# Residual and stores of the first half beside its inverse, a second store queue and a third PSUM pair at the end of an S4 and MLP mixer

## The chip, the cores and the metric

The kernel runs on one core of a Trainium2 chip. Its engines are TensorE (PE), VectorE (DVE), ScalarE (ACT), GpSimd (POOL) and SyncE (SP), each with an instruction stream of its own; they meet through semaphores. SP only issues DMAs here. PE writes PSUM (eight banks of 128 partitions x 2 KB), the other work happens in SBUF, and inputs, output and scratch are in HBM. The metric is the device time of one execution in microseconds, as a median of several.

## What is computed: the reference, cut short

```python
def reference(A_u, ...):
    x = A_u                                   # (1, 2048, 512) f32
    xn = _layernorm(x)
    s = _A_ref(xn, ...)      # S4: K[d, l] = Re sum_n C exp(dt A l) dt B
                             # s = irfft(rfft(xn) * rfft(K)) + xn * Dskip
    g = _silu(_B_ref(xn, B_w1, B_w2, B_w3, B_w4))
    return x + s * g

def _B_ref(x, w1, w2, w3, w4):
    h = _gelu(_layernorm(x) @ w1)             # 512 -> 512
    x1 = x + shift(h) @ w2                    # four channel groups moved by +1, -1, +2, -2 rows
    return x1 + _gelu(_layernorm(x1) @ w3) @ w4   # 512 -> 1376 -> 512
```

The convolution along the 2048 positions, its kernel K, the MLP, the gate and the residual are all within the time.

## The kernel before

**Layout.** X is one SBUF tile of [128, 16, 512] f32: position index (t r s) has s (16 values) in the middle dimension and (r t) on the 128 partitions; the channels are split into two halves of DH = 256 (hf = 0 and 1). X holds the normalized input first, then x1, then the MLP's result, then its Silu, then the product with the convolution, and at last the sum that is stored.

**Stages, as the program lists them.** (1) `loads`, `params`, `token_mixing`: the inputs come in, the first MLP (w1, w2) runs, the input of the convolution goes to DRAM as scr_Ud, and w3, w4 are cut into f16 parts. (2) `tables(hf)`: 16 blocks of 32 channels make the convolution's kernel. ACT computes exponentials (mag) and sines, DVE forms the tables pt and kt (128x2080), PE sums them in pc, and the result goes to scr_Kd. (3) `kstage1(hf)` loads ksl from scr_Kd, transforms it (`pd<-ksl,ks`), copies it to k1e and stores scr_Kf. (4) `products(hf)`: loads kin, uin and cst; PE transforms, DVE multiplies the spectra (pr), PE goes half way back (`pd<-pr,cst`), copies z1e are stored to scr_Zda or scr_Zdb. (5) `mlp(g)`, g = 0 to 7, each for two values of s (1024 columns of X): `pb<-x1T,w3h` matmuls in f16, Gelu to g, g rounded into f16 ghl and its remainder, `pa<-w4h,ghl` matmuls, and `X<-pa,wsc,X` adds them to X. (6) `gate(g)`: Silu on ACT, 128x1024. (7) `inverse(hf, g)`, 16 units: one DMA loads zin, 16 matmuls `p?<-zin,is` fill a pair of PSUM banks, and two DVE products of 128x256 multiply X by them. Such a unit of 16 matmuls with its pair of products is what the text calls a unit. The pair of banks comes from `pp_pair`, which alternates between banks 2 and 3, named pc and pd (pc0, pc1 are the two tiles of one pair). (8) `finish(g)`: every second g loads x again into xr ([128, 4, 512], four DMAs by `by_r`, one per group of 32 partitions), DVE adds 128x1024 of it to X, and four DMAs store the result to out_dram, all on SP's queue Q.

**What sets the order.** None of this is issued as written. `Plan` records every instruction with its reads and writes, and `Plan.order` is a list scheduler: it simulates the engines with planned costs (`pe_cost`, `act_cost`, `dve_cost`, 0.45 us for a DMA issue on SP, LAND for a transfer's landing), and of the instructions that are ready gives each engine the one with the lowest due time. A due time is the base of a stage (T0 + TC * cc for a table block, M0 + MC * g for an MLP group, KA, KB, PA, PB, FA, FB for the others) plus an entry of SHIFT, which has one number for each call of `due`. Copies and some roundings (`E.copy`, `E.affine`) may go to ACT or DVE; PREFER and AVOID say which. So an instruction's place comes from numbers, and each engine then runs its stream in that order. In the profile every instruction carries the line of the helper that issues it, L310 before and L314 after; instructions are told apart by their tiles.

**Places that the text speaks of.** `pp_pair` (line 559), `due` (571), `by_r` (577), `inverse` (893), `finish` (910), the rings of buffers zinr and the places xrs (543, 544). zinr[0] has five buffers of 4 KB per partition for the zin of the first half, zinr[1] eight for the second.

Of the kernel before, what the change touches and what calls it, by code (L numbers as in the profile page):

```python
# [10 lines left out]
F32 = mybir.dt.float32  # L11
# [8 lines left out]
P = 128  # L20
L = 2048
D = 512
# [61 lines left out]
class Op:  # L84
# [10 lines left out]
SAME = {"PE": 0.0, "ACT": 0.13, "DVE": 0.1, "SP": 0.0}  # L95
TABLE_LOAD = 1.41
DMA_RATE = 300e3
LAND, PAD = 2.45, 0.16
BASE, FINE, END = 16512, 19840, 229368

KGC, QUAD = 3.25, 0.95
WARM = 40

SHIFT = (
# [21 lines left out]
)  # L126
Q0, QC = -778.0, 0.05
SWITCH = 2279.26
PREFERP, AVOIDP = 2674.41, 272.51
PREFER, AVOID = 3332.92, 790.65  # L130
PV, T0, TC = 257.0, 396.7, 309.52
LX, LC, LP, LW, LV = -4000.0, 0.11, -3964.6, -2693.7, -3696.7
M0, MC, WC = 807.9, 710.86, 0.25
H0, HC, SC = -3530.1, 638.4, 0.22
KA, PA, PAC, FA = -1045.1, -3015.7, 0.25, 592.1
KB, PB, PBC, FB = -157.1, -136.4, 0.08, 323.0
FC = 0.29


def mlp_due(g, jp):  # L140
# [3 lines left out]
class Plan:  # L144
# [105 lines left out]
    def order(self):  # L250
# [17 lines left out]
        while len(out) < len(ops):  # L268
# [4 lines left out]
            for o in pools[e]:  # L273
                if o.ready <= t + 0.02:
                    v = o.vt
                    if e == "ACT" and o.table and o.table != table:
                        v += SWITCH
                    if len(o.alts) > 1:
# [37 lines left out]
def is_ap(x):  # L316
    return hasattr(x, "tensor") and hasattr(x, "ap")


def columns(ap):  # L320
    n = 1
    for s in ap.shape[1:]:
        n *= s
    return n


def pe_cost(name, args):
    f = 1 if args[2].dtype == F16 else 4
    return 0.11 if name == "transpose" else columns(args[2]) * f / 2400.0 + 0.0025 * (1 + f // 4)


def act_cost(args, kw):
    small = sum(1 for k in ("bias", "scale") if is_ap(kw.get(k)))
    cost = columns(args[0]) * (0.00075 if "PSUM" in str(args[1].space) else 0.00084) + 0.092 + 0.088 * small
    return cost + (0.11 if is_ap(kw.get("accum_out")) else 0.0)
# [19 lines left out]
class Engine:  # L355
# [3 lines left out]
    def __getattr__(self, name):  # L359
        def call(*args, **kw):  # L360
            aps = [a for a in args if is_ap(a)] + [kw[k] for k in ("bias", "scale") if is_ap(kw.get(k))]
            writes, reads = aps[:1], aps[1:]
            if is_ap(kw.get("accum_out")):
                writes = writes + [kw["accum_out"]]
            if name == "matmul" and not kw["start"]:
                reads = reads + writes
            table, nbytes = 0, 0
            if self.eng == "PE":
                cost = pe_cost(name, args)
            elif self.eng == "ACT":  # L370
                cost = act_cost(args, kw)
                if name == "activation":
                    table = TABLES.get(args[2], 0)
            elif self.eng == "DVE":
                cost = dve_cost(name, args)
            else:
                cost = 0.45
                nbytes = 4 * min(columns(a) * a.shape[0] for a in aps)
            self.plan.add({self.eng: (cost, (name, args, kw))}, writes, reads, table, nbytes)

        return call
# [38 lines left out]
def kernel(  # L420
# [9 lines left out]
    V, A, T, Q = [Engine(plan, e) for e in ("DVE", "ACT", "PE", "SP")]  # L430
    E = Either(plan)

    xv = u[0].rearrange("(t r s) d -> r t s d", r=4, s=S)
    ov = out[0].rearrange("(t r s) d -> r t s d", r=4, s=S)
# [5 lines left out]
    DH = D // 2  # L440
# [13 lines left out]
    def at(offset, shape, dt, name):  # L454
        return nc.alloc_sbuf_tensor_at(name, shape, dt, offset=offset)[:]
# [37 lines left out]
    X = at(area(4 * S * D), [P, S, D], F32, "X")  # L493
    K2, K4 = 2048, 4096
# [8 lines left out]
    early = area(11 * K2)  # L503
# [25 lines left out]
    o = late + 8 * K4  # L529
# [10 lines left out]
        ),  # L540
    ]

    zinr = [Ring(early, K4, 5), Ring(o, K4, 8)]
    xrs = [late + 2 * K4 * k for k in range(3)] + [o + 10 * K4]
    assert o + 12 * K4 <= END

# [1 line left out]
    bank = [[ps.tile([P, D], F32, name=f"p{n}{i}") for i in range(2)] for n in "abcd"]  # L548
    turn = {"mm": 0, "kg": 0, "pp": 0, "t": 0}
# [6 lines left out]
        turn["kg"] += 1  # L556
        return bank[2][turn["kg"] % 2]

    def pp_pair():
        turn["pp"] += 1  # L560
        return bank[2 + turn["pp"] % 2]

    def t_bank():
        turn["t"] += 1
# [6 lines left out]
    def due(t=None):  # L571
        plan.stage += 1
        t = plan.base = plan.base if t is None else t
        plan.vt = t + (SHIFT[plan.stage] if plan.stage < len(SHIFT) else 0)


    def by_r(sb, dr, to_dram=False):

        for r in range(4):
            a, d = sb[32 * r : 32 * r + 32], dr[r]  # L580
            Q.dma_start(d, a) if to_dram else Q.dma_start(a, d)

    w1s, w2s = [], []

# [303 lines left out]
    def gate(g):  # L888
        due(FA + FC * g)
        X2 = X[:, 2 * g : 2 * g + 2]  # L890
        A.activation(X2, X2, AF.Silu)

    def inverse(hf, g):
        due((FA, FB)[hf] + FC * g)
        ch = slice(hf * DH, hf * DH + DH)
        zin = zinr[hf]([P, 4, DH], F32, "zin")
        Q.dma_start(zin, Zd[hf][:, 2 * g : 2 * g + 2, :, :, :].rearrange("r s e g d -> (s e g) r d"))
        py = [t[:, :DH] for t in pp_pair()]
        with plan.together(cost=0.55):
            for r in range(4):  # L900
                for a in range(2):
                    h = slice(64 * a, 64 * a + 64)
                    T.matmul(py[a][32 * r : 32 * r + 32], is2[h], zin[h, r], start=True, stop=True)
        for a in range(2):
            Xh = X[:, 2 * g + a, ch]
            V.tensor_mul(Xh, Xh, py[a])

    xr = []

    def finish(g):  # L910
        due(FB + FC * g)
        if g % 2 == 0:
            xr.append(at(xrs.pop(), [P, 4, D], F32, "xr"))
            by_r(xr[-1], xv[:, :, 2 * g : 2 * g + 4])
        X2 = X[:, 2 * g : 2 * g + 2]
        V.tensor_add(X2, X2, xr[-1][:, 2 * (g % 2) : 2 * (g % 2) + 2])
        by_r(X2, ov[:, :, 2 * g : 2 * g + 2], to_dram=True)


    def pow2_scale(cols, dst_s, dst_inv, target):  # L920
# [296 lines left out]
    for hf in range(2):  # L1217
        for g in range(8):
            inverse(hf, g)
    for g in range(8):  # L1220
        finish(g)
    with nc.allow_non_contiguous_dma(reason="parameters by state"), tc.manual_schedule():
# [26 lines left out]
```

## Time and profile before

| quantity | value |
| --- | --- |
| median of 3 runs | 673.19 us (671.51 to 675.04) |
| time of the profiled execution | 671.43 us |
| its span in the profile | 669.7 us |
| PE busy | 629.2 us, 94% of the span |
| DVE busy | 540.2 us, 81% |
| ACT busy | 479.8 us, 72% |
| HBM read and written | 61.16 MB and 33.55 MB |
| mean DMA rate | 141 GB/s over the span |

The span is the time from the first to the last event of the profiled execution; the device time has some 1.7 us more. A row of the timeline gives start and length in us, engine, line, operation, the tile written and those read, the shape and how many instructions were put together; in brackets stands the idle time of the engine before it and what ended it. PEclk is the granted clock of TensorE as a share of its full 2.4 GHz.

### The profile page before, as it was taken

Reading aid. Unit: us, or ns where it says so; the run is one execution under the profiler, and the core shown is the slowest. Engines: PE = TensorE matmul, PEld = TensorE weight load, DVE = VectorE, ACT = ScalarE, POOL = GpSimd, SP = SyncE. Lnnn points to the kernel's source line nnn. Section 1 sums busy time; section 2 is a strip of 40 time slices with the busy share of each in tenths; the row PEclk is TensorE's granted clock in tenths of the full one; section 3 lists DMA queues with packets and bytes.
Section 4 is the critical chain, followed back from the end, with each engine's and each line's share of the span. In section 5 each row is a group of like instructions: output and inputs, shape, how many; then the busy total and the mean of one; then the engine's idle time right before and its main releaser. Section 6 shows DMA issues by size and latency. Waiting matters only on the chain.

```text
span 669.7 us, 13855 instructions
## 1 busy us (share of the span) xinstructions
PE 629.2 (94%) x5526; PEld 416.4 (62%) x5526; DVE 540.2 (81%) x798; ACT 479.8 (72%) x1050; POOL 0.7 (0%) x6
## 2 busy tenths in 40 slices
PE   7699989999995998998999999999999999999984
PEld 7567758466464785665687576676675756556531
DVE  5898999999999999988999999997434155454557
ACT  3989899969849999987999999994245363223420
POOL 0000000000000000000000000000000000000000
PEclk9899979999997999998999999999999999999995
DMA  8945342421022120385343314328599468844997
GB/s 258 244 132 188 107 162 93 144 98 55 32 80 79 32 61 21 80 221 173 78 137 100 97 60 125 103 75 211 168 249 276 135 148 215 205 155 142 236 315 219
DMA packets 98063, 95.60 MB, mean 143 GB/s; under 512 B 48272, under 2 KB 77968, under 8 KB 97104
## 3 DMA queue, kind: packets, MB, share of 16 engines
q1 hardware_dynamic: 98000, 94.73, 50.2%
q8 instruction: 43, 0.70, 0.4%
q14 instruction: 20, 0.16, 0.1%
HBM read 61.16 MB, written 33.55 MB: 141 GB/s over the span
## 4 chain that ended last, share of the span: by engine, by line
PE 54%; DVE 32%; DMA 6%; ACT 4%; issue 3%; SPq 1%; DVEq 0%; ACTq 0%
PE pb L310 19%; PE pa L310 12%; PE pc L310 12%; PE pd L310 11%; DVE pt L310 10%; DVE X L310 4%; DVE kt L310 4%; DMA X<-in_A_u_dram 2%; DVE pr L310 2%; DVE ghl L310 2%; DVE stats L310 2%; DVE eg L310 2%; DMA zin<-scr_Zda 1%; SPq L310 1%; DVE pab L310 1%
## 5 line engine op out<-in xcount | busy, mean ns | idle before, releaser
L310 PE MATMUL pb<-x1T,w3h 128*128 128x256 f16 (+1 forms) x1056 | 126.0, 275 | 1.1 <-DVE w3h L310 1.1
L310 PE MATMUL pa<-w4h,ghl 128*128 128x512 f16 (+1 forms) x528 | 124.5, 383 | 1.1 <-DVE w4h L310 0.8
L310 PEld LDWEIGHTS <-w3h 128*128 128x128 f16 (+1 forms) x1056 | 102.8, 101 | 30.2 <-issue 15.4
L310 ACT ACT_TABLE_LOAD x85 | 109.1, 1283 | 2.5 <-PEq L1237 0.7
L310 PEld LDWEIGHTS <-ghl 128*128 128x128 f16 (+1 forms) x528 | 49.2, 98 | 67.5 <-issue 16.2
L310 ACT ACTIVATE mag<-par 128x64 f32<-128x64 f32 x512 | 84.0, 272 | 6.3 <-DVE pt L310 6.1
L310 PE MATMUL pc<-kt 128*32 128x64 f32 x1024 | 84.6, 415 | 0.6 <-DVE kt L310 0.6
L310 PE MATMUL pc<-pt 128*32 128x64 f32 x1024 | 78.4, 387 | 0.0
L310 PE MATMUL pb<-xT,w 128*128 128x256 f32 x256 | 61.1, 396 | 1.4 <-ACT hT L310 1.4
L310 DVE SCALAR_TENSOR_TENSOR ghl<-g,wsc,ghl 128x512 f16<-128x512 f32 (+1 forms) x48 | 35.3, 750 | 31.0 <-ACT ghl L310 30.7
L310 PEld LDWEIGHTS pb<-xT,w 128*128 128x128 f32 x256 | 50.0, 199 | 15.8 <-issue 6.8
L310 PEld LDWEIGHTS pc<-pt 128*32 128x32 f32 x1024 | 56.8, 194 | 0.1
L310 PEld LDWEIGHTS pc<-kt 128*32 128x32 f32 x1024 | 48.8, 175 | 9.6 <-issue 6.2
L310 ACT ACTIVATE g<-pb,wsc 128x512 f32<-128x512 f32 (+1 forms) x48 | 32.8, 692 | 26.8 <-PE pb L310 26.5
L310 ACT ACTIVATE ghl<-g,wsc 128x512 f16<-128x512 f32 (+1 forms) x32 | 22.6, 714 | 27.0 <-PE pa L310 26.9
L310 DVE TENSOR_TENSOR kt<-mag,kt 128x1024 f32<-128x1024 f32 x32 | 41.6, 1300 | 0.0
L310 DVE SCALAR_TENSOR_TENSOR pt<-kt,pt 128x2080 f32<-128x2080 f32 x16 | 37.7, 2359 | 0.1
L310 ACT COPY z1e<-pd 128x256 f32<-128x256 f32 x36 | 12.7, 389 | 34.0 <-PE pd L310 34.0
L310 DVE TENSOR_TENSOR pr<-pc,kh 128x512 f32<-128x512 f32 x32 | 21.0, 686 | 19.4 <-PE pc L310 16.7
L310 PE MATMUL pd<-pr,cst 64*128 64x256 f32 x256 | 36.3, 402 | 0.0
L310 ACT ACTIVATE kt<-kt,halfpi 128x2080 f32<-128x2080 f32 x16 | 33.0, 2063 | 0.0
L310 DVE COPY z1e<-pd 128x256 f32<-128x256 f32 x28 | 11.6, 441 | 25.9 <-PE pd L310 25.9
(159 smaller groups left out, 990.7 us busy)
## 6 DMA issues: line engine op xcount, KB each, us to landing
wst<-in_B_w_dram SPq DMA_DIRECT2D x20, 512.0 KB, 3.7
scr_Ud<-ue SPq DMA_DIRECT2D x16, 512.0 KB, 3.1
scr_Kfa<-k1e SPq DMA_DIRECT2D x16, 256.0 KB, 3.6
uin<-scr_Ud SPq DMA_DIRECT2D x32, 128.0 KB, 3.1
cst<-c_gp SPq DMA_DIRECT2D x16, 256.0 KB, 2.8
kin<-scr_Kfa SPq DMA_DIRECT2D x32, 128.0 KB, 2.7
scr_Zda<-z1e SPq DMA_DIRECT2D x16, 256.0 KB, 2.3
xr<-in_A_u_dram SPq DMA_DIRECT2D x16, 256.0 KB, 6.3
```

What stands on the lines that cost most here:

```text
L310: ins = [getattr(self.engines[op.eng], name)(*args, **kw).ins for name, args, kw in op.calls]
```

## The change

Four edits and a new set of numbers:

- The residual of the first 256 channels gets a function of its own, `finish_first(g)`, called behind `inverse(0, g)`: it loads half a row of x into a new tile xh ([128, 2, 256], ring xhr of five buffers of 2 KB), adds it and stores the half on SP's queue. `finish(g)` keeps the second half. The ring of zin for the first half is cut from five buffers to three to make room.
- `by_r` may use two queues: the stores of `finish` alternate between SP's queue and ACT's.
- `pp_pair` cycles through three pairs (banks 1, 2, 3: pb, pc, pd) for the inverse units of the second half with g > 1.
- A DMA issue on ACT is planned at 0.45 us, and LAND is 2.64 instead of 2.45.
- All due times (SHIFT and the constants of the bases) are new.

```diff
-LAND, PAD = 2.45, 0.16
+LAND, PAD = 2.64, 0.16
...
 SHIFT = (
-    -2357, -12777, -7728, -8471, -1890, -5820, 626, 2299, 7826, 2606, 3103, -2484, -1642, 1374, 635, 1552,
...
+    -12647, -27352, -19672, -6255, 707, -6201, 3977, 27896, 32956, 28997, -2982, -46821, 11292, -6043, -15837,
...
-KB, PB, PBC, FB = -157.1, -136.4, 0.08, 323.0
-FC = 0.29
+KB, PB, PBC, FB = -11129.1, 4798.2, 0.06, -47696.6
+FC = 0.08
...
-                cost = act_cost(args, kw)
+                cost = 0.45 if name == "dma_start" else act_cost(args, kw)
...
-    zinr = [Ring(early, K4, 5), Ring(o, K4, 8)]
+    zinr = [Ring(early, K4, 3), Ring(o, K4, 8)]
+    xhr = Ring(early + 3 * K4, K2, 5)
...
-    def pp_pair():
+    def pp_pair(last):
         turn["pp"] += 1
-        return bank[2 + turn["pp"] % 2]
+        return bank[1 + turn["pp"] % 3] if last else bank[2 + turn["pp"] % 2]
...
-    def by_r(sb, dr, to_dram=False):
+    def by_r(sb, dr, to_dram=False, queues=(Q, Q)):
...
-            Q.dma_start(d, a) if to_dram else Q.dma_start(a, d)
+            queues[r % 2].dma_start(d, a) if to_dram else Q.dma_start(a, d)
...
-        py = [t[:, :DH] for t in pp_pair()]
+        py = [t[:, :DH] for t in pp_pair(hf == 1 and g > 1)]
...
+    def finish_first(g):
+        due(FA + FC * g)
+        x = xhr([P, 2, DH], F32, "xh")
+        by_r(x, xv[:, :, 2 * g : 2 * g + 2, :DH])
+        X2 = X[:, 2 * g : 2 * g + 2, :DH]
+        V.tensor_add(X2, X2, x)
+        by_r(X2, ov[:, :, 2 * g : 2 * g + 2, :DH], to_dram=True)
...
     def finish(g):
         due(FB + FC * g)
         if g % 2 == 0:
-            xr.append(at(xrs.pop(), [P, 4, D], F32, "xr"))
-            by_r(xr[-1], xv[:, :, 2 * g : 2 * g + 4])
-        X2 = X[:, 2 * g : 2 * g + 2]
+            xr.append(at(xrs.pop(), [P, 4, DH], F32, "xr"))
+            by_r(xr[-1], xv[:, :, 2 * g : 2 * g + 4, DH:])
+        X2 = X[:, 2 * g : 2 * g + 2, DH:]
         V.tensor_add(X2, X2, xr[-1][:, 2 * (g % 2) : 2 * (g % 2) + 2])
-        by_r(X2, ov[:, :, 2 * g : 2 * g + 2], to_dram=True)
+        by_r(X2, ov[:, :, 2 * g : 2 * g + 2, DH:], to_dram=True, queues=(Q, A))
...
             inverse(hf, g)
+            if hf == 0:
+                finish_first(g)
```

**DVE at the end.** From the second of the last two MLP accumulations on (X_90 is X, pa1 the MLP's PSUM tile, xr and xh the loaded x, pc and pd the PSUM pairs of the inverse). Before:

```order
L310 SCALAR_TENSOR_TENSOR X_90<-pa1_94,wsc_79,X_90 128x512
L310 TENSOR_TENSOR X_90<-X_90,xr_652 128x1024
L310 TENSOR_TENSOR X_90<-X_90,pd0_99 128x256
L310 TENSOR_TENSOR X_90<-X_90,pd1_100 128x256
L310 TENSOR_TENSOR X_90<-X_90,xr_653 128x1024
L310 TENSOR_TENSOR X_90<-X_90,pc0_97 128x256
L310 TENSOR_TENSOR X_90<-X_90,pc1_98 128x256
```

After:

```order
L314 SCALAR_TENSOR_TENSOR X_90<-pa1_94,wsc_79,X_90 128x512
L314 TENSOR_TENSOR X_90<-X_90,xr_660 128x2x256
L314 TENSOR_TENSOR X_90<-X_90,pd0_99 128x256
L314 TENSOR_TENSOR X_90<-X_90,pd1_100 128x256
L314 TENSOR_TENSOR X_90<-X_90,xr_661 128x2x256
L314 TENSOR_TENSOR X_90<-X_90,pc0_97 128x256
L314 TENSOR_TENSOR X_90<-X_90,pc1_98 128x256
L314 TENSOR_TENSOR X_90<-X_90,xh_650 128x2x256
```

The additions have half their columns, and one of them (xh_650) belongs to the first half of the last Silu's piece. Behind these rows come, each with its addition of xr, a pair from pd and four from pc before, and three from pc after. The third pair of banks, pb, does not appear: in both orders the last four pairs of products are from pc.

**ACT at the end.** Its last instructions (g32 is g, the Gelu's result; ghl its f16 rounding). Before:

```order
L310 ACTIVATE g32_547<-pb0_95,wsc_79 96x256
L310 ACTIVATE ghl_544<-g32_543,wsc_79 128x512
L310 ACTIVATE ghl_546<-g32_545,wsc_79 128x512
L310 ACTIVATE ghl_548<-g32_547,wsc_79 96x256
L310 ACT_TABLE_LOAD
L310 ACTIVATE X_90<-X_90 128x1024
```

After:

```order
L314 ACTIVATE g32_545<-pb1_96,wsc_79 128x512
L314 ACTIVATE g32_547<-pb0_95,wsc_79 96x256
L314 ACTIVATE ghl_544<-g32_543,wsc_79 128x512
L314 DMA out_0_dram<-X_90 32x2x256 x2
L314 ACTIVATE ghl_548<-g32_547,wsc_79 96x256
L314 DMA out_0_dram<-X_90 32x2x256 x4
L314 ACT_TABLE_LOAD
L314 ACTIVATE X_90<-X_90 128x1024
L314 DMA out_0_dram<-X_90 32x2x256 x10
```

Sixteen stores now stand in ACT's stream, two of them ahead of the last rounding ghl_548 and six ahead of the last table load and the Silu of the last MLP group.

**SP between the table loads ksl and the loads kin of the second half** (scr_Zda are stored first-half products, zin their loads, scr_Kfb the stores of k1e). Before:

```order
L310 DMA scr_Zda_65<-z1e_402 128x512
L310 DMA zin_635<-scr_Zda_65 128x4x256
L310 DMA zin_639<-scr_Zda_65 128x4x256
L310 DMA zin_638<-scr_Zda_65 128x4x256
L310 DMA zin_637<-scr_Zda_65 128x4x256
L310 DMA zin_636<-scr_Zda_65 128x4x256
L310 DMA scr_Kfb_64<-k1e_550 64x2x1024 x2
L310 DMA scr_Kfb_64<-k1e_551 64x2x1024 x2
L310 DMA scr_Kfb_64<-k1e_553 64x2x1024 x2
L310 DMA scr_Kfb_64<-k1e_554 64x2x1024 x2
L310 DMA kin_557<-scr_Kfb_64 128x4x64 x4
```

After:

```order
L314 DMA xh_644<-in_A_u_dram 32x2x256 x4
L314 DMA xh_640<-in_A_u_dram 32x2x256
L314 DMA scr_Zda_65<-z1e_402 128x512
L314 DMA xh_640<-in_A_u_dram 32x2x256 x3
L314 DMA xh_638<-in_A_u_dram 32x2x256 x4
L314 DMA xh_636<-in_A_u_dram 32x2x256 x2
L314 DMA zin_639<-scr_Zda_65 128x4x256
L314 DMA xh_642<-in_A_u_dram 32x2x256 x2
L314 DMA scr_Kfb_64<-k1e_550 64x2x1024 x2
L314 DMA scr_Kfb_64<-k1e_551 64x2x1024 x2
L314 DMA xh_642<-in_A_u_dram 32x2x256 x2
L314 DMA zin_637<-scr_Zda_65 128x4x256
```

Twenty loads of xh are threaded in from just before ksl to the last stores of k1e (18 of them in these rows), and of the five loads of zin three are left here, behind most of them; two have gone out of this stretch.

## Rows read from the trace of the kernel before

**Rows 1.** The page, busy time, share of the span and instructions of each engine
```profile
PE 629.2 (94%) x5526; PEld 416.4 (62%) x5526; DVE 540.2 (81%) x798; ACT 479.8 (72%) x1050; POOL 0.7 (0%) x6
```

**Rows 2.** Windows: stretch, length, busy (instructions) of PE, PEld, DVE, ACT, POOL; PEclk, DMA, GB/s
```profile
80.00:100.00 20.00, 16.95 (x144) 11.09 (x146) 20.00 (x20) 18.79 (x20) 0.00 (x0) 0.83 0.47 160
300.00:320.00 20.00, 18.18 (x190) 10.93 (x189) 18.27 (x22) 15.21 (x71) 0.00 (x0) 0.91 0.56 161
440.00:460.00 20.00, 20.00 (x266) 15.34 (x266) 19.64 (x25) 16.43 (x17) 0.00 (x0) 1.00 0.51 141
625.00:635.00 10.00, 9.51 (x118) 5.11 (x123) 5.56 (x13) 5.50 (x6) 0.00 (x0) 1.00 1.02 236
650.00:669.70 19.70, 7.71 (x97) 2.22 (x96) 14.72 (x24) 1.06 (x1) 0.00 (x0) 0.60 0.76 212
```

**Rows 3.** Timeline of PE round 308 us and round 400 us
```profile
307.48 1.09 PE L310 MATMUL pd<-ksl,ks 32*64 32x512 f32 x8 [1.82 <-DMA uin<-scr_Ud]
308.50 4.45 PE L310 MATMUL pa<-w4h,ghl 128*128 128x512 f16 x12
...
399.62 0.66 PE L310 MATMUL pb<-ident,x1n 128*128 128x128 f32 x4 [0.20 <-ACT g L310]
```

**Rows 4.** Timeline of PE, DVE and ACT in the last 26 us
```profile
644.06 0.66 PE L310 MATMUL pc<-zin,is 64*32 64x256 f32 x16
...
646.65 2.77 PE L310 MATMUL pa<-w4h,ghl 128*128 128x512 f16 x12
...
650.77 0.74 DVE L310 SCALAR_TENSOR_TENSOR X<-pa,wsc,X 128x512 f32<-128x512 f32 x1
...
651.54 1.06 ACT L310 ACTIVATE X<-X 128x1024 f32<-128x1024 f32 x1 [6.86 <-DVE X L310]
...
657.07 0.74 DVE L310 TENSOR_TENSOR X<-X,pc 128x256 f32<-128x256 f32 x2
...
657.53 1.43 PE L310 MATMUL pc<-zin,is 64*32 64x256 f32 x16 [1.15 <-DVE X L310]
...
659.04 0.75 DVE L310 TENSOR_TENSOR X<-X,pc 128x256 f32<-128x256 f32 x2
...
663.80 1.23 DVE L310 TENSOR_TENSOR X<-X,xr 128x1024 f32<-128x1024 f32 x1
```

**Rows 5.** Groups by form: engine, operation, tiles, form, count; busy us, mean ns; idle before
```profile
L310 PE MATMUL pb<-x1T,w3h 128*128 128x256 f16 x960 | 114.4, 275 | 0.1
L310 PE MATMUL pa<-w4h,ghl 128*128 128x512 f16 x480 | 113.1, 384 | 0.3 <-DVE ghl L310 0.3
...
L310 DVE TENSOR_TENSOR X<-X,xr 128x1024 f32<-128x1024 f32 x8 | 9.8, 1224 | 0.2
...
L310 PE MATMUL pb<-ident,x1n 128*128 128x128 f32 x48 | 7.2, 280 | 0.2 <-ACT g L310 0.2
L310 DVE TENSOR_SCALAR ghl<-g,wsc 128x512 f16<-128x512 f32 x13 | 7.2, 556 | 2.6 <-PE pa L310 2.1 <-ACT g L310 0.5
...
L310 DVE TENSOR_TENSOR tm<-tm 128x512 f32<-128x512 f32 x3 | 2.1, 687 | 0.0
```

**Rows 6.** The tile of the output: issues on SP (ns, shortest, median, longest), landing
```profile
L310 SPq DMA_DIRECT2D out_dram<-X x32: 314/421/938, 648.8 to 666.4; - x32
...
DMA to landing us min/median/max: 1.9/2.2/2.4
```

**Rows 7.** Windows of 5 us, before and behind the end of the MLP
```profile
640.00:645.00 5.00, 5.00 (x50) 1.86 (x49) 1.90 (x4) 2.51 (x3) 0.00 (x0) 1.00 1.10 349
660.00:665.00 5.00, 2.38 (x32) 0.46 (x25) 4.93 (x7) 0.00 (x0) 0.00 (x0) 0.50 0.90 266
```

**Rows 8.** Timeline of SP's queue from 488 us, and the loads of xr
```profile
488.48 4.02 SPq L310 DMA_DIRECT2D ksl<-scr_Kdb  x2
...
501.20 2.73 SPq L310 DMA_DIRECT2D zin<-scr_Zda  x5
510.15 19.49 SPq L310 DMA_DIRECT2D scr_Kfb<-k1e  x8
...
615.55 8.64 SPq L310 DMA_DIRECT2D xr<-in_A_u_dram  x8
```

More of the change, by code (lines that the diff above doesn't have):

```diff
@@ L104 @@
 SHIFT = (
[21 rows of a table removed]
-)
[L127 to L135, printed above, removed]
-KB, PB, PBC, FB = -157.1, -136.4, 0.08, 323.0
-FC = 0.29
[25 rows of a table added]
+)
+Q0, QC = -12452.7, 0.16
+SWITCH = 10178.4
+PREFERP, AVOIDP = 16413.8, -27136.7
+PREFER, AVOID = 30928.3, 17051.7
+PV, T0, TC = 1064.1, 7968.3, 2351.02
+LX, LC, LP, LW, LV = -4000.0, 1.75, -20967.6, 79.7, 38767.4
+M0, MC, WC = 11445.2, 7647.32, 0.05
+H0, HC, SC = 9720.0, 0.11, 0.09
+KA, PA, PAC, FA = -15294.9, -53917.9, 0.05, 30977.6
+KB, PB, PBC, FB = -11129.1, 4798.2, 0.06, -47696.6
+FC = 0.08
 def mlp_due(g, jp):
```

44 rows, old and new, of the table SHIFT are left out of this document.

## The prediction

> **What bounds the kernel now.** I read the busy times first [rows 1]: TensorE (PE) 94% of the span, VectorE (DVE) 81%, ScalarE (ACT) 72%. Such means hide the stages, so the table of windows comes next [rows 2], and in it three regimes. From about 80 to 457 us DVE is full (20.00 of 20 in the first of these windows, 19.64 in the last) and ACT nearly so; PE is filled round it. From 313 us PE is full as well, and from 457 to 649 PE alone is the bound. The timeline of PE shows where the last loss of the middle lies: a wait of 1.82 us at 307.48, and 12 MLP matmuls behind it that take 4.45 us instead of some 2.77 [rows 3, 4]; from there to the end of the MLP PE waits for 0.2 us in all. The third regime is the end. The last MLP matmuls end at 646.65 + 2.77 = 649.42 us [rows 4]; call this T. What follows is no PE time: of the 19.70 us from 650 on PE works 7.71, DVE 14.72 [rows 2]. DVE multiplies the last pieces by the gate, adds the residual (1.23 us for one pair of tiles), and ends its last addition at 663.80 + 1.23 = 665.03 = T + 15.6; the span ends at 669.7 = T + 20.3.
>
> The execution profiled took 671.43 us for a span of 669.7, so 1.73 lie outside. The median of the runs is 673.19. I sum against the span and carry the difference of 1.76 between the two times over to the median.
>
> **The residual of the first half.** Eight additions of 1024 columns become sixteen of 512. One of 1024 costs 1.22 us and one of 512, by the nearest row (a DVE product of 128x512), 0.69 [rows 5]; between half the first (0.61) and this I take 0.65. That is 0.6 us more work for DVE in all. But by the order seven of the eight first-half additions stand ahead of the MLP's last accumulations, where DVE works 5.56 us of 10 [rows 2]: PE's matmuls hide them. Without that cover they would cost 7 x 0.65 = 4.6 us, what they cost now. One, for pieces 14 and 15, has to wait for the last Silu and stays behind T.
>
> **The end, step by step.** Up to the second accumulation nothing changes: it ends at 650.77 + 0.74 = T + 2.1 [rows 4], and Silu at 651.54 + 1.06 = T + 3.2. In the order of after DVE then has addition, pair of products, addition (0.65 + 0.75 + 0.65, T + 4.1); the pair of the last Silu's piece, ready by then; and four additions with three more pairs between them. Those three and the piece before them all lie in one PSUM pair, pc, in spite of the third pair: the first two units behind T alone change banks. So each waits as now: PE starts 0.46 us after DVE's pair began (657.07 to 657.53), takes 1.43, and DVE's next pair starts 0.08 later at 659.04, a round of 1.97 [rows 4]. Today DVE fills that round itself (0.75 + 1.23); with a short addition it does not, and PSUM sets it. Three rounds from T + 4.1 give T + 10.0, the last pair and addition 0.75 + 0.65: T + 11.4. At the higher clock a unit took 0.66 us before T (of 1.43), DVE's 1.35 would set the round, and it would be T + 9.5; the lower level is what the trace shows there (1.43 at the last units), so I take 11.4.
>
> Behind the last addition lie 4.67 us today: four issues on one queue, a landing of 2.2 us and the close. Two queues issue two each, which saves two issues of 0.42 [rows 6] and their gaps: -0.9. If an issue on ACT, which this trace does not have, costs as much as SP's longest, 0.94 [rows 6], half of that is gone; it could also be as cheap as 0.31. I take SP's median. The end is then T + 11.4 + 3.8 = T + 15.2 for T + 20.3: **-5.1 us**. Bounds: -7.0 with the higher clock, -4.4 with slow issues and additions of 0.69.
>
> One thing goes back. Six units instead of seven stand behind T, so one of 0.6 us moves in front of it: **+0.6**.
>
> On the second queue the rows are plain: while the stores run, the DMA engines are busy at 0.90 of their time with 266 GB/s [rows 7], and I count the queue at issue time alone. The Trainium skill ("DMA: Bandwidth & Descriptors", section "Issuing engines are not separate DMA queues") says the same of any such split: DMAs from several engines run on the same 16 engines, and only the sequencer's time is saved. Had I counted the queue as double rate, the end would be some 2 us shorter; by that sentence it is not, and where the stores pile up it would bring nothing at all, which is the third rival.
>
> **ACT's queue.** Two stores stand ahead of the last piece of the MLP (ghl_548 behind a wait for DVE's addition of xr_660). Behind that wait ACT has ghl_548, which DVE and PE's last six matmuls need. By PE's rows between (a unit 0.66, MLP groups of 12 at 2.77) the addition is done some 3 us before PE gets there, so I count nothing; without that cover it is the excess over 3 us.
>
> **Loads.** x is read in 48 DMAs instead of 16, so SP issues 32 more, 20 of them between the table load ksl and the loads kin of the second half. A queue entry costs 0.42; 20 are 8.4 us. SP has that time: between ksl's issue, ended 492.5, and the first store of k1e at 510.15 it issues little but five loads of zin [rows 8], two of which are gone. PE's work between the last matmul on ksl and the first on kin is 20.4 us in the new order, 18.4 in the old: nothing counted. The first-half stores go out while PE works.
>
> **Due times.** Every number is new, and the orders agree in only half to two thirds of their rows, so I weigh what each engine has in front of it. At the eleventh of the 16 blocks of tables, whose matmuls start right behind PE's last loss in the trace, DVE has 4.7 us less to do first (six first roundings of ghl of 0.56, four normalizations, six copies gone to ACT, against two roundings of kt and one subtraction more; each at its form's mean less the overlap), and PE has 12 + 12 MLP matmuls and four transposes less done, which are 12 x 0.236 + 12 x 0.119 + 4 x 0.15 = 4.9 us [rows 5]. DVE arrives 4.7 earlier, PE has 4.9 more left: +0.2, call it 0. At the 16th block the new order has some 10 us more slack, but before shows no wait of PE there, so this buys nothing. The loss before it is not visible from an order; I keep it, with bounds of 4 us either way (somewhat over twice the 1.82 of rows 3).
>
> Sum: -5.1 + 0.6 + 0 = -4.5. Span 665.2, profiled time 666.9, median 673.19 - 4.5 = **668.7 us**.
>
> **The rivals.** (1) The middle gains too. The 1.82 us of waiting and the 1.68 us of slow matmuls at 307 us [rows 3] go with the new order: another -3.5, 665.2. For it: ACT's new order starts the exponentials of the seventh block earlier, and ACT idles 4.8 of 20 us around there [rows 2]. Against: DVE's total arrives no earlier in relation to PE.
> (2) Slower: SP's queue becomes the bound at 480 to 530 us. An issue of xr took 1.08 us when DMA was full (8 in 8.64) [rows 8]. At that pace 20 xh loads take 21.6 us, 13.2 over my 8.4; the idle time of SP there, 510.15 - 492.5 less 3 = 14.6, holds the 8.4 and some 6 more, so k1e's stores, kin and PE come 7 us late: +7.0 - 4.5 = 675.7. It decides from about 0.73 us per issue. Against: an xr load has 256 KB, an xh load 64.
> (3) The gain at the end is lost. If the loads of zin hold the stores back until T, 4.19 MB at 266 GB/s are 15.8 us, and with landing and close the end is at T + 19: 672.5. For it: DMA moves at the full 349 GB/s until 645 [rows 7]. Against: the last product unit stands 12 us earlier in PE's order, so zin is read earlier. If ACT sets the middle's pace instead of DVE (its work up to the eleventh block falls by only 0.5 us), PE's 4.9 us come back as +4.4, about the same time.
>
> **How the numbers follow.** Forecast 0.50, middle gains 0.20, end lost or ACT bound 0.18, SP bound 0.12. The forecast's own range is 665 to 672. A change of 0.5%, 3.4 us, is about what a measurement of this kernel can tell from none: faster is below 669.8. Of the forecast some 0.38 lies there, with all of the first rival 0.58, and a little of the third: 0.60. Slower (over 676.6) has part of the second and of larger losses in the middle, 0.12; the rest, 0.28, is within. The range takes in the first rival with the higher clock and reaches into the second: 661.0 to 675.5.
>
> **What would show it.** Right: the last addition about 11 us behind the last MLP matmul, the span's end 15 behind it; the last units of zin 2 us apart with DVE idle in each round; first-half stores issued before the MLP's end; T at 649 to 651. Wrong: T beyond 653 (then look for PE waiting on kin or ksl at 485 to 535, or DVE on ACT's sines at 290 to 350); stores still queued on SP when the last addition is done; ACT's ghl_548 late behind its two stores.

## The result, and the profile after

The changed kernel takes 675.45 us (median of 18 runs, 673.32 to 678.34), the kernel before, run beside it, 672.21 us: a ratio of 1.0043, 95% interval 1.0031 to 1.0056. It is slower by 0.4%, some 3 us, where 668.7 and a gain were forecast. The profiled execution has a span of 674.8 us for 669.7 before.

The page's first line for after, to be held beside [rows 1]: PE has the same work (628.5 for 629.2 us), DVE 6 us less.

```profile
PE 628.5 (93%) x5526; PEld 418.0 (62%) x5526; DVE 533.8 (79%) x786; ACT 479.0 (71%) x1062; POOL 0.7 (0%) x6
```

The end tells the rest. The timeline of after, PE, DVE and the two queues (SPq and ACTq are the DMA issues of SP and of ACT; start, length and count of a run of issues with their waits):

```profile
638.59 10.24 SPq L314 DMA_DIRECT2D out_dram<-X  x12
...
647.57 2.77 PE L314 MATMUL pa<-w4h,ghl 128*128 128x512 f16 x12
...
648.93 0.38 SPq L314 DMA_DIRECT2D zin<-scr_Zda  x1
649.36 23.02 SPq L314 DMA_DIRECT2D out_dram<-X  x36
...
653.41 0.67 PE L314 MATMUL pc<-zin,is 64*32 64x256 f32 x16 [2.49 <-DMA zin<-scr_Zda]
...
656.11 8.25 ACTq L314 DMA_DIRECT2D out_dram<-X  x10
...
656.46 1.43 PE L314 MATMUL pc<-zin,is 64*32 64x256 f32 x16 [1.95 <-DVE X L314]
...
658.44 1.43 PE L314 MATMUL pc<-zin,is 64*32 64x256 f32 x16 [0.55 <-DVE X L314]
...
662.73 0.69 DVE L314 TENSOR_TENSOR X<-X,xr 128x512 f32<-128x512 f32 x1
```

The last MLP matmuls end at 647.57 + 2.77 = 650.34 (T; before 649.42, [rows 4]). The units of 1.43 us stand 1.98 apart as foreseen, after a wait of 2.49 for the load of zin issued at 648.93. The last addition is done at 662.73 + 0.69 = 663.42, T + 13.1; before it was T + 15.6. And yet the span ends 11.4 us later, at T + 24.5: SP is issuing stores until 649.36 + 23.02 = 672.38. Behind the last addition lay 4.7 us before.

SP's queue, whose rows of before are [rows 6, 8], shows how it came to be late. First three of its rows from 614 us on, then what it waited for from 612 us to the end (us in total, times, longest):

```profile
614.02 0.36 SPq L314 DMA_DIRECT2D scr_Zdb<-z1e  x1
...
622.82 7.45 SPq L314 DMA_DIRECT2D zin<-scr_Zdb  x7
...
634.47 0.38 SPq L314 DMA_DIRECT2D zin<-scr_Zdb  x1
```

```profile
SPq L314 <- DMA out_dram<-X: 9.2, 6, 3.1
SPq L314 <- DMA zin<-scr_Zdb: 4.6, 2, 3.7
...
SPq L314 <- DVE X L314: 0.6, 2, 0.4
```

At 614 SP begins on the loads of xh and zin; seven loads of zin alone take 7.45 us. From 614.02 to 672.38 it has 74 entries and 58.4 us for them. The additions to which the first 24 stores belong are done between 613.58 + 0.69 and 632.01 + 0.68:

```profile
613.58 0.69 DVE L314 TENSOR_TENSOR X<-X,xh 128x512 f32<-128x512 f32 x1
...
632.01 0.68 DVE L314 TENSOR_TENSOR X<-X,xh 128x512 f32<-128x512 f32 x1
```

but the first store leaves at 638.59, because in SP's order all of them stand behind these loads. The 3.7 us between the last of the loads (634.47 + 0.38 = 634.85) and the first store are a wait too, for an earlier load of zin to land: the store takes the semaphore that this load still held (how the semaphores go round is told under e1). From 638.59 on 49 entries take until 672.38, 33.8 us or 0.69 each. Of these 33.8, 9.2 are waits on `out_dram<-X`, other stores, 1.1 a wait on one more load of zin, and only 0.6 are waits on DVE's additions; without the waits an entry takes 0.47. DMA itself had room (windows of 10 us; the last two columns are the busy share of the DMA engines and GB/s):

```profile
650.00:660.00 10.00, 4.89 (x82) 1.48 (x80) 6.78 (x15) 2.34 (x2) 0.00 (x0) 0.77 0.73 190
660.00:670.00 10.00, 1.43 (x16) 0.40 (x16) 2.85 (x6) 0.00 (x0) 0.00 (x0) 0.50 0.52 132
```

### The profile page after: what moved, and what is told of

It is laid out like the page before. It is cut to its first block, busy times and chain, and to the rows that moved or that the text cites. A ratio compares the mean times of both kernels' runs of the same rounds, so it can differ in the third digit from the quotient of the medians.

```text
span 674.8 us, 13933 instructions
## 1 busy us (share of the span) xinstructions
PE 628.5 (93%) x5526; PEld 418.0 (62%) x5526; DVE 533.8 (79%) x786; ACT 479.0 (71%) x1062; POOL 0.7 (0%) x6
## 4 chain that ended last, share of the span: by engine, by line
PE 45%; DVE 32%; DMA 8%; ACT 6%; issue 5%; SPq 3%; DVEq 0%; ACTq 0%
PE pb L314 16%; PE pa L314 12%; DVE pt L314 11%; PE pd L314 9%; PE pc L314 8%; DVE kt L314 6%; DVE X L314 3%; SPq L314 3%; DMA X<-in_A_u_dram 2%; DVE pr L314 2%; DVE stats L314 2%; ACT kt L314 2%; DMA ksl<-scr_Kdb 2%; DVE eg L314 2%; DVE pab L314 1%
## 5 line engine op out<-in xcount | busy, mean ns | idle before, releaser
L314 PE MATMUL pa<-w4h,ghl 128*128 128x512 f16 (+1 forms) x528 | 122.3, 380 | 2.4 <-DVE ghl L314 2.4
L314 PEld LDWEIGHTS pb<-xT,w 128*128 128x128 f32 x256 | 50.1, 200 | 15.2 <-issue 4.8
L314 ACT ACTIVATE ghl<-g,wsc 128x512 f16<-128x512 f32 (+1 forms) x42 | 29.3, 713 | 22.6 <-PE pa L314 22.3
L314 ACT ACTIVATE kt<-kt,halfpi 128x2080 f32<-128x2080 f32 x16 | 33.8, 2115 | 0.0
L314 ACT COPY z1e<-pd 128x256 f32<-128x256 f32 x38 | 13.4, 386 | 28.5 <-PE pd L314 20.3
L314 DVE TENSOR_TENSOR pr<-pd,kh 128x512 f32<-128x512 f32 x32 | 24.1, 767 | 9.8 <-PE pd L314 6.7
```

Source lines behind the costliest of these rows:

```text
L314: ins = [getattr(self.engines[op.eng], name)(*args, **kw).ins for name, args, kw in op.calls]
```

## The experiments

T is the end of the last MLP matmuls, the last three columns before the ratio are of the profiled execution. Ratios are to the kernel before, run on the same chip beside each.

| kernel | stores on SP, ACT | T | last addition | end of span | ratio (95% interval) |
| --- | --- | --- | --- | --- | --- |
| before | 32, 0 | 649.42 | T + 15.6 | T + 20.3 | 1 |
| after | 48, 16 | 650.34 | T + 13.1 | T + 24.5 | 1.0043 (1.0031 to 1.0056) |
| e9, before with the new numbers | 32, 0 | 651.79 | T + 15.6 | T + 20.2 | 0.9999 (0.9986 to 1.0011) |
| e8, before with two queues | 16, 16 | 650.89 | T + 15.6 | T + 20.6 | 1.0000 (0.9986 to 1.0013) |
| e3, after, last zin first | 48, 16 | 650.62 | T + 11.0 | T + 24.1 | 1.0055 (1.0039 to 1.0072) |
| e1, after, one queue | 64, 0 | 648.63 | T + 11.0 | T + 22.2 | 1.0016 (0.9997 to 1.0036) |
| e6, after, ACT never waits | 48, 16 | 646.97 | T + 11.3 | T + 20.6 | 0.9981 (0.9964 to 0.9999) |
| e2, after, early stores on ACT | 24, 40 | 661.67 | T + 11.4 | T + 15.2 | 1.0079 (1.0053 to 1.0105) |
| e11, e1 with 48 stores | 48, 0 | 651.71 | T + 11.4 | T + 16.7 | 0.9941 (0.9920 to 0.9962) |
| e4, after, whole rows | 16, 16 | 650.21 | T + 10.9 | T + 16.2 | 0.9927 (0.9902 to 0.9953) |
| e5, e4 on one queue | 32, 0 | 650.67 | T + 10.5 | T + 15.3 | 0.9916 (0.9902 to 0.9929) |
| e10, e5 with two PSUM pairs | 32, 0 | 649.60 | T + 15.3 | T + 20.4 | 0.9960 (0.9944 to 0.9975) |
| e7, e5 with pairs in PE's order | 32, 0 | 651.09 | T + 7.3 | T + 12.2 | 0.9880 (0.9862 to 0.9897) |

T is no sharp measure: e1, e3 and e6 have the same order of PE and DVE as after until close to the end, and T lies between 646.97 and 650.62 in them. The distances from T are what the profiles give, the medians of the ratios the rest.

My theory on reading the trace: the end is set by SP's queue, by the number of stores (64 instead of 32) and by waits. The rivals: the late load of zin; the waits of SP on stores that ACT has still to send; the DMA engines with half rows; the new due times.

**e9: the new numbers alone.** The kernel before with SHIFT, all constants and LAND of after, the stage counter moved on where `finish_first` would call `due`:

```diff
             inverse(hf, g)
+            if hf == 0:
+                due()
```

> The kernel before with nothing but the new numbers (SHIFT, the constants, LAND). Stores as the cause: the last MLP matmul ends near 650, some 0 to 1.5 us later than before's 649.4, the end lies some 20 us behind it, the span is 670 to 671. Due times as the cause of the slowdown: the end lies over 23 us behind the last MLP matmul or that matmul ends later than 652.

The ratio is 0.9999. The due times neither gain nor lose, and the end has its old shape. All of the change lies in the other edits.

**e3: the late zin.** In the planned order the last load of zin is moved ahead of the 12 stores that stand before it on SP (e1, e2, e3 and e6 keep the order planned for after and move single entries of it, in `Plan.issue`):

```diff
-        for op in self.order():
+        out = self.order()
+        stores = [op for op in out if store_of(op)][:12]
...
+        k = out.index(last) + 1
+        out[k:k] = stores
+        for op in out:
```

> The changed kernel with the last zin load (zin_649) moved on SP's queue in front of the 12 stores that stand ahead of it. Late zin theory: the last addition comes 2.5 us earlier and the end too, 2.5 us faster than after. Queue theory: the last addition 2.5 us earlier, but 49 issues stand on SP from 638.6 as before, so the end moves by 0 to 1 us, up to 2.5 only as far as SP waits for additions.

SP and the last addition, timeline of e3:

```profile
657.84 14.45 SPq L322 DMA_DIRECT2D out_dram<-X  x26
...
660.91 0.69 DVE L322 TENSOR_TENSOR X<-X,xr 128x512 f32<-128x512 f32 x1
```

The addition is done at 661.60, T + 11.0 instead of T + 13.1, and the end does not move: SP is at its stores until 657.84 + 14.45 = 672.29. The late zin cost the last addition 2 us and the kernel nothing that the runs show.

**e1: all stores on SP.**

```diff
+        for op in out:
+            if store_of(op):
+                op.eng = "SP"
```

> The changed kernel with its planned order kept and the 16 stores of ACT's queue issued from SP at their places. Queue theory (the end is set by SP issuing some 0.48 us per store: 15 of its stores are still to be issued when the last addition is done at 663.4): 52 instead of 36 stores stand behind the last zin load, 16 x 0.48 = 7.7 us more issue, less the up to 3.4 us that SP now waits for stores of ACT: span some 4 us longer than the 674.8 of after, 2 to 8. Rival, waits across the queues (SP is held by semaphores that ACT's stores still occupy): as fast or up to 3 us faster. Rival, the late load of zin_649: no change.

SP's rows and waits in e1:

```profile
632.18 9.70 SPq L318 DMA_DIRECT2D out_dram<-X  x12
641.98 0.38 SPq L318 DMA_DIRECT2D zin<-scr_Zda  x1
642.41 25.99 SPq L318 DMA_DIRECT2D out_dram<-X  x52
```

```profile
SPq L318 <- DMA zin<-scr_Zdb: 3.2, 4, 1.3
SPq L318 <- DMA zin<-scr_Zda: 2.1, 3, 1.2
SPq L1273 <- DMA out_dram<-X: 1.3, 2, 0.8
...
SPq L318 <- DVE X L318: 0.2, 1, 0.2
```

Against the count theory's expectation, 64 stores on one queue are faster than 48 and 16 on two: 1.0016 for 1.0043. The last 52 take 25.99 us, 0.50 each, and no store waits for another store any more (the 1.3 us belong to the close, the program's last waits, line 1273). After's 36 took 0.64 each. So the second queue does harm here, by waits; how much is not sharp, since the two intervals overlap a little (1.0031 to 1.0036). e3, which also has two queues and ran on the same chip as e1, lies clear of it (from 1.0039).

What waits is seen in three records of after (start, length, queue, and the number of the semaphore that the store takes; the DMAs of both queues take eight semaphores in turn, and one must have landed before its semaphore is taken again):

```
659.71 0.32 SP  store, semaphore 101
661.47 0.32 ACT store, semaphore 102
663.11 0.32 SP  store, waits for semaphore 102 and takes it
```

ACT's store had to wait for an addition that ended at 661.43; SP's next store, whose data were ready, waited 3.1 us for ACT's to be issued and to land. By the same records 8.9 of after's 9.2 us are waits on stores that ACT issued. A load holds its semaphore in the same way: most of the waits on zin in the rows of e1 are its first stores waiting for loads of zin to land.

**e6: ACT's stores never wait.** All second-half stores go to SP, and ACT issues, behind its last Silu, 16 first-half stores that are long ready. The numbers on the queues are those of after.

```diff
+        for op in out:
+            if store_of(op):
+                op.eng = "SP"
+        early = [op for op in out if store_of(op)][:16]
...
+        out[k:k] = early
```

> The changed kernel with its planned order, but the 16 stores of ACT's queue exchanged: all second-half stores are issued from SP, and ACT issues, in one row behind its last Silu, the 16 first-half stores that are ready first. SP still has 48 stores, ACT 16, but no store on ACT waits for a late addition. Waits across the queues as the cause of the end (in after SP stood 8.7 us waiting for semaphores of stores that ACT had not yet sent or that had not landed): those waits go, 48 issues take 23 us from some 636 on, only a few stores lie behind the last addition and the span is 6 to 9 us shorter than after's 674.8. Count alone (48 issues on SP, whoever waits): no change within 1 us.

```profile
640.36 24.83 SPq L324 DMA_DIRECT2D out_dram<-X  x41
...
649.10 8.00 ACTq L324 DMA_DIRECT2D out_dram<-X  x16
```

```profile
SPq L324 <- DMA out_dram<-X: 3.6, 1, 3.6
SPq L324 <- DVE X L324: 2.3, 5, 0.8
```

0.9981 for 1.0043: 0.6%, some 4 us, go with the waits, less than the 6 to 9 expected. One wait of 3.6 us on another store is left (ACT's 16 stand behind a Silu that starts at 649.10), and the count stays: at T + 11.3 SP still has 14 stores. Both parts of the theory hold, neither alone.

**e11: fewer stores, same pieces.** e1, with the first half stored for two g at once:

```diff
-        by_r(X2, ov[:, :, 2 * g : 2 * g + 2, :DH], to_dram=True)
+        if g % 2:
+            by_r(X[:, 2 * g - 2 : 2 * g + 2, :DH], ov[:, :, 2 * g - 2 : 2 * g + 2, :DH], to_dram=True)
```

> The changed kernel with all stores on SP (as e1), and the first half stored for two pieces of g at once: 16 stores of 32x4x256 instead of 32 of 32x2x256, so 48 in all instead of 64, still half rows in the same 1 KB pieces. Count theory: 16 issues of 0.47 us less, 7.5 us, which is about all that e1's queue is late; the end is then some 15 to 17 us behind the last MLP matmul, 5 to 7 us shorter than e1, ratio to before 0.992 to 0.995. If the 1 KB pieces or DMA throughput make half rows slow, the same bytes in the same pieces give no change: ratio 0.999 to 1.002.

The stores of e1 and of e11 (issue times, first and last start):

```profile
L318 SPq DMA_DIRECT2D out_dram<-X x64: 315/432/1500, 632.2 to 668.0; - x64
```

```profile
L314 SPq DMA_DIRECT2D out_dram<-X x48: 315/429/1612, 635.5 to 665.6; - x48
```

0.9941 for e1's 1.0016, the end at T + 16.7 for T + 22.2. The bytes and the 1 KB pieces are the same, 16 issues are gone, and 5.5 us with them. It is the count that costs. This pair is the cleanest of the study: six units stand behind T in both, and the last additions lie 0.4 us apart.

**e4 and e5: whole rows.** The additions stay split; a piece is stored in rows of 512 channels once its second half is done, from two queues (e4) or one (e5, without `queues=(Q, A)`):

```diff
-        by_r(X2, ov[:, :, 2 * g : 2 * g + 2, :DH], to_dram=True)
...
-        by_r(X2, ov[:, :, 2 * g : 2 * g + 2, DH:], to_dram=True, queues=(Q, A))
+        by_r(X[:, 2 * g : 2 * g + 2], ov[:, :, 2 * g : 2 * g + 2], to_dram=True, queues=(Q, A))
```

> The changed kernel without the stores of the first half alone: the additions stay split, and a piece is stored in whole rows (32x1024) once its second half is done, still alternating between SP and ACT. 32 stores instead of 64. Queue theory: 16 on each queue, none waits behind the last addition, the end some 15 to 16 us behind the last MLP matmul, 8 to 9 us faster than after. DMA throughput theory: 4.2 MB still go out from 640 on, at the 266 GB/s seen before some 16 us, end some 17 us behind: 7 us faster. Late due times in the middle as the cause: the last MLP matmul stays at 650 and nothing else changes.

> e4 (whole rows, 32 stores) with all stores on SP's queue. Count theory (each store costs its queue 0.47 us, and the second queue takes half of them): the last four are issued one behind the other, 1.9 us instead of 0.95, so the span is 1 us longer than e4's 666.4, at 667.4, and some more if stores pile up before. Waits across the queues as the main cost: no longer than e4, up to 1 us shorter.

Timeline of e5 at the end, and SP's wait for DVE:

```profile
645.46 17.69 SPq L314 DMA_DIRECT2D out_dram<-X  x28
...
649.20 1.47 PE L314 MATMUL pa<-w4h,ghl 96*128 96x512 f16 x6
...
654.42 1.25 PE L314 MATMUL pc<-zin,is 64*32 64x256 f32 x16 [3.16 <-DVE X L314]
...
656.18 1.43 PE L314 MATMUL pc<-zin,is 64*32 64x256 f32 x16 [0.51 <-DVE X L314]
...
660.46 0.69 DVE L314 TENSOR_TENSOR X<-X,xr 128x512 f32<-128x512 f32 x1
```

```profile
SPq L314 <- DVE X L314: 11.1, 8, 3.9
```

Now SP waits for DVE, 11.1 us in all, as a queue with time to spare does; T is 649.20 + 1.47 = 650.67, the last addition T + 10.5, the end T + 15.3. Both kernels are faster than before by 0.7 to 0.8%. The second queue again brings nothing: e5 is no slower than e4. But the number of stores is not all that differs from after: by a count of PE's units the planner, which orders these kernels anew, leaves four of them behind T in e4 and e5, where after and e1 have six. The last addition of e5 is 0.5 us nearer to T than e1's.

**e8: the second queue alone.**

```diff
-        by_r(X2, ov[:, :, 2 * g : 2 * g + 2], to_dram=True)
+        by_r(X2, ov[:, :, 2 * g : 2 * g + 2], to_dram=True, queues=(Q, A))
```

> The kernel before with nothing but its 32 stores alternating between SP and ACT (PE and DVE in the same order). Count theory: the four issues behind the last addition become two and two, 0.9 us shorter than before. Waits across the queues: they cost something here too, since ACT's stores wait for additions in the same way: between 0.9 shorter and 2 us longer, the end then more than 3.8 us behind the last addition.

The tile of the output in e8 (issue times, then from issue to landing), beside [rows 6]:

```profile
L310 SPq DMA_DIRECT2D out_dram<-X x16: 314/380/489, 650.3 to 666.9; - x16
L310 ACTq DMA_DIRECT2D out_dram<-X x16: 366/414/446, 650.3 to 667.0; - x16
...
DMA to landing us min/median/max: 2.0/3.3/3.7
```

The last stores are issued sooner, but a store lands after 3.3 us instead of 2.2. The 0.9 us that I counted are eaten by that, ratio 1.0000. The Trainium skill ("DMA: Bandwidth & Descriptors", section "Issuing engines are not separate DMA queues") says that DMAs from several engines interleave on the same 16 DMA engines and only sequencer time is saved; these rows agree, and add that here the landing pays for it.

**e2: early stores on ACT.**

```diff
+        for op in [op for op in out if store_of(op)][:24]:
+            op.eng = "ACT"
```

> The changed kernel with its planned order kept, the first 24 stores (first half, pieces whose addition is done by 632) issued from ACT instead of SP. Queue theory: 24 stores instead of 48 are left on SP, no store waits behind the last addition, and the end falls from 24.5 us behind the last MLP matmul to some 15 to 17: 7 to 9 us faster than after. Late zin_649 alone: it is issued 10 us earlier, the last addition comes 2.5 us earlier, and so does the end: 2.5 us faster. Small descriptors or DMA throughput as the limit: no change, since the same bytes go out in the same pieces.

ACT and PE in e2:

```profile
637.83 6.63 ACTq L318 DMA_DIRECT2D out_dram<-X  x5
644.55 1.28 ACT L318 ACT_TABLE_LOAD   x1 [5.85 <-DMA out_dram<-X]
...
645.85 0.69 ACT L318 ACTIVATE g<-pb,wsc 128x512 f32<-128x512 f32 x1
```

```profile
635.66 2.54 PE L318 MATMUL pa<-w4h,ghl 128*128 128x512 f16 x11
647.76 1.11 PE L318 MATMUL pb<-zin,is 64*32 64x256 f32 x16 [9.57 <-ACT g L318]
```

The end is as expected, T + 15.2, and the kernel is slower all the same: five stores hold ACT for 6.63 us, the table and the Gelu behind them come at 644.55 and 645.85, and PE waits 9.57 us for that g. T slips to 661.67, and so the end is no proof of the theory here: SP had some 11 us more for its stores. By the records the five issues themselves take 1.8 of the 6.63 us; the rest are waits for semaphores, two of which were held by loads of zin from SP's queue, landed at 642.37 and 644.12. The Trainium skill ("DMA: Bandwidth & Descriptors", section "Anatomy of one DMA — SWDGE (gpsimd) path") says that any wait of a DMA for a semaphore happens on the issuing sequencer. Its section is on DMAs issued from GpSimd; the trace shows the same for ACT with these 6.63 us.

**e10 and e7: the PSUM pairs.** e10 is e5 with the two pairs of before; e7 deals three pairs to the last units in the order in which PE reaches them:

```diff
-        py = [t[:, :DH] for t in pp_pair(hf == 1 and g > 1)]
+        py = [t[:, :DH] for t in pp_pair({1: 1, 2: 0, 3: 0, 4: 2, 5: 0, 6: 0, 7: 3}.get(g) if hf else None)]
```

> e5 with the PSUM pairs of before (pc and pd in turn, no pb). The forecast gave the third pair no gain at the end but one unit moved in front of the last MLP matmul. Seven units instead of six stand behind it now: one round of 1.98 us more behind, 0.6 us less in front, span 1.4 us longer than e5's 666.0. If the third pair does nothing: no change within 0.5 us.

> e5 (whole rows, one queue) with the PSUM pairs of the last units dealt out in the order in which PE reaches them (g = 1 to pb, 4 to pc, 7 to pd). The planner then puts two more units in front of the last MLP matmul (+1.2 us there), and behind it no unit waits for its bank in a round of 1.98 us. By the rows of e5: last addition some 6.6 us behind the last MLP matmul instead of 10, end some 11.5 behind instead of 15.3, span 2 to 3 us shorter than e5's 666.0. If SP's queue still sets the end (32 stores of 0.47 us from some 640 on), no more than 1 us.

e10, then e7:

```profile
648.13 1.47 PE L314 MATMUL pa<-w4h,ghl 96*128 96x512 f16 x6
...
649.36 17.49 SPq L314 DMA_DIRECT2D out_dram<-X  x32
...
652.68 1.44 PE L314 MATMUL pd<-zin,is 64*32 64x256 f32 x16 [0.93 <-DVE X L314]
...
657.91 1.44 PE L314 MATMUL pc<-zin,is 64*32 64x256 f32 x16 [0.55 <-DVE X L314]
...
664.18 0.69 DVE L314 TENSOR_TENSOR X<-X,xr 128x512 f32<-128x512 f32 x1
```

```profile
645.15 15.22 SPq L314 DMA_DIRECT2D out_dram<-X  x28
...
649.62 1.47 PE L314 MATMUL pa<-w4h,ghl 96*128 96x512 f16 x6
...
651.02 0.66 PE L314 MATMUL pd<-zin,is 64*32 64x256 f32 x16
...
654.83 2.04 PE L314 MATMUL pc<-zin,is 64*32 64x256 f32 x16 [3.15 <-DVE X L314]
...
657.73 0.69 DVE L314 TENSOR_TENSOR X<-X,xr 128x512 f32<-128x512 f32 x1
```

With two pairs seven units stand behind T (e5 has four, not the six that I had counted on), and rounds of 1.98 us, one behind the other, bring the last addition to T + 15.3, where before had it (T + 15.6) with additions twice as long: 0.44% slower than e5, 3 us for the 1.4 expected. One thing stays open. e10's end is no shorter than before's, T + 20.4 for T + 20.3, and yet its runs are faster, 670.37 us for 673.01, with an interval clear of 1. If the runs have the same distance behind T as the profiled executions, these 2.6 us lie ahead of T; the profiled execution of e10 (671.84 us) does not show them, and no run here says where they come from. With the pairs in turn only one unit (654.83) waits behind T and the last addition is done at T + 7.3. e7, 664.73 us (663.74 to 667.21) for 673.01, is the fastest kernel of this study, 1.2% below before.

## Why the prediction was wrong, point by point

- **The middle, 0 (bounds 4):** right as far as the new numbers go: e9 gives 0.9999. The unit moved in front of T (0.6 us) is within the scatter of T. Rival 1, a gain there, is not seen: PE's wait for uin did fall from 1.8 to 0.3 us, but one of 2.4 us for ghl (before 0.3) and one of 1.9 for pt came instead. e10 leaves open whether the shorter additions give something in the middle.
- **The last addition, T + 11.4:** nearly right: T + 13.1, of which 2 us are the late zin (e3: T + 11.0). The rounds of 1.98 us came as priced. I gave the third pair no part in it; by e10, planned with two pairs, the shorter additions would have gained nothing there without it.
- **Behind the last addition, 3.8 us:** wrong, and this is the step that failed. It took SP's queue to be empty but for the last piece's stores. It was 11.4 us: by the records 18 of SP's stores are issued after the last addition has ended, and two of them belong to it.
- **"The first-half stores go out while PE works":** the error behind it. The order has all of them behind all but the last of the loads of zin, and I priced the queue at 0.42 an entry for 480 to 530 us, where it had room, and not for the last 60 us, where it had none. A sum like that for the end would have shown how tight it was: 48 stores at 0.47 are 23 us, and their last comes with the last addition only if the first leaves 23 us ahead of it and nothing waits. In after the first left 24.8 us ahead of it (638.59 to 663.42), so that the count alone had next to no room; the 10.9 us of waits are what made SP late by so much.
- **The second queue, -0.9:** wrong in sign. Alone it gains nothing (e8); in this change it costs 0.27% (e1 against after, two intervals that overlap a little), since stores of ACT that wait for additions hold semaphores that SP's stores need next.
- **ACT's queue, nothing:** right in after (PE does not wait for ghl_548), but only as long as few stores stand there; e2 shows the price.
- **Loads at 480 to 530:** right, PE waits 0.8 us in all from 420 to 650, so rival 2 fell there; its mechanism, SP's queue as the bound, was the true one 130 us later. Its 675.7 is the nearest of the forecast times to the 675.45 measured, and 675.45 lies just inside the range of 661.0 to 675.5, which was drawn into this rival; both are luck, since the loads that it priced cost nothing.
- **Rival 3, the end's gain lost, 672.5:** nearest in what it says of the end, with the wrong reason. It had the stores limited by 266 GB/s. In after DMA moved 132 to 190 GB/s with a quarter to a half of its time free; the issues and the waits between them were the limit.

In sum, by the ratios: the structure with whole rows is worth -0.84% (e5), storing 64 half rows instead of 32 rows +1.0% (e1 against e5, with the two units that e5 has ahead of T), the second queue +0.27% (the least certain of the three). Together they are +0.43%, the measured change, as they must be, since each step starts from the kernel at which the one before ended. e5's end, T + 15.3, is nearly the one forecast for after (T + 15.2), but with four units behind T instead of the six in the forecast.

## What to carry to other kernels

Count the entries of a DMA queue, loads and stores with their issue time, over the stretch in which they have to leave, just as an engine's work is counted; splitting stores doubles that term, whatever the bytes. A store that waits for data does not wait alone: it holds the instructions behind it on its engine and, through semaphores used in turn, the stores of another queue. Look at where the trace has the queue's last issue against the last addition before pricing what comes behind it.

## What the runs showed of the hardware that was not expected

DMAs of SP and ACT take the same eight semaphores in turn in these kernels, so that SP stood 8.9 us in after for stores of the other queue and none in e1. A store of 128 KB in whole rows landed after 2.2 to 2.5 us when one queue issued them (before, e5, e10, e7), after 3.0 (e4) to 3.3 us (e8) when two did. A load of zin (512 KB) took SP about 1 us to issue while others were in flight (7 in 7.45 us), where a store took 0.43 (medians of the stores in after).
